# Twenty-seven tiny extra loads in a softmax-attention kernel: fifteen on SyncE near the end, twelve on GpSimd at head 22

## The chip, the cores and the metric

The kernel runs on one core of a Trainium2 chip. The metric is the device time of one launch in microseconds. A profile of a separate execution, taken by the hardware profiler, shows where the time goes; its span is counted from the first to the last instruction.

## What is computed

One decode step of full attention and its gradients, for 32 heads, one query row per head, 8192 keys and values of 128 elements, all in bf16:

```python
def _fwd_reference(q, k, v):
    scale = q.shape[-1] ** -0.5
    scores = jnp.einsum('bhqd,bhkd->bhqk', q, k) * scale
    attn = _softmax(scores, axis=-1)
    return jnp.einsum('bhqk,bhkd->bhqd', attn, v)

def reference(q, k, v, grad_out):
    _out, _vjp = jax.vjp(_fwd_reference, q, k, v)
    return (_out, *_vjp(grad_out))
```

K and V are read once (2 MB a head each) and dK and dV, of the same size, are written once. dV of a head is the outer product of its 8192 probabilities with its row of `grad_out`; dK is that of the 8192 score gradients with its row of `q`. The outputs `out_0` (attention) and `out_1` (dQ) are 8 KB each.

## The kernel before

**Tiles.** A head's K, V, dK or dV is one tile of 128 partitions by 64 rows by 128 elements in bf16: 16 KB a partition, contiguous in memory. There are three buffers for K (`K_BUFS`), two for V (`V_BUFS`), and two each for dK and dV (pool `gen`).

**The loop.** The loop over `h` runs from 0 to 32 and is skewed by one head: in turn `h` the scores, softmax and output of head `h` are computed, and dK and dQ of head `h - 1` are finished. TensorE makes the scores and the contractions, VectorE transposes K blocks in 32x32 squares (`k_blocks`) and makes the outer products (`outer`, a quarter of a tile at a time), ScalarE copies and takes the exponential.

**Order.** From `manual_schedule()` on, every engine's instructions, its queue of transfers too, stand in the order in which the program names them. In a turn, SyncE's queue gets: the load of K of head `h + 2` (L336), the store of dK of head `h - 1` (behind the last quarter, L365), the load of V of head `h + 2` (L390) and the store of dV of head `h` (L391). Head 0 and head 31 store in halves; K of head 0 comes in four pieces. Two transfers are issued by ScalarE: the rows of `q` and `grad_out` at the start (L88, L89). The first load of K, V, K, V (heads 0 and 1, L90 to L93) stands before the hand-made order begins. For the last heads no load is left: V of head 31 is asked for in turn 29. Turn 30 therefore ends with the store of dV of head 30; turn 31 then stores dK of 30, dV of 31 in halves and the attention result (`result`, L395), and turn 32 stores dK of 31 in halves and the dQ result (L397).

**GpSimd** clears some tiles at the start and has nothing to do after that; it issues no transfer.

Lines that matter: L81 loads K, L85 loads V, L266 stores dK and dV, L302 stores a result, L424 is the end of the program.

Of the kernel before, what the change touches and what calls it, by code (L numbers as in the profile page):

```python
# [11 lines left out]
BF16 = mybir.dt.bfloat16  # L12
# [7 lines left out]
K_BUFS = 3  # L20
V_BUFS = 2
QD = 32


@with_exitstack
def kernel(
# [11 lines left out]
    nc = tc.nc  # L38
    P = 128
    _, H, S, D = k.shape  # L40
    assert D == P and S % (P * CH) == 0 and H <= P
    NT = S // P
    NCH = NT // CH
    NQ = P // QD
    assert NCH == 4 and NQ == 4
    W = D // 2
    NB = W // QD
    scale = float(D) ** -0.5
# [8 lines left out]
    single = ctx.enter_context(tc.tile_pool(name="single", bufs=1))  # L57
# [11 lines left out]
    def rows_of(x, h, c, parts):  # L69
        L = NT // parts  # L70
        return x[0, h].rearrange("(p n) d -> p n d", p=P)[:, c * L:(c + 1) * L, :]
# [11 lines left out]
    def load_v(h):  # L83
        Vt[h] = vpool.tile([P, NT, D], BF16, tag="V", name="Vt")
        nc.sync.dma_start(Vt[h][:], rows_of(v, h, 0, 1))  # L85
# [16 lines left out]
    nc.vector.memset(ones_f[:], 1.0)  # L102
    do_win = consts.tile([P, H, 2, QD + 2], BF16)
    nc.gpsimd.memset(do_win[:], 0.0)
    wins = {}
    for which in ("p", "ds"):
        wins[which] = []
        for i in range(2):
            w = consts.tile([P, NG, 2 * QD - 4], BF16, name=f"win_{which}{i}")
            nc.gpsimd.memset(w[:], 0.0)  # L110
            wins[which].append(w)
    q_win = []
    for i in range(2):
        w = consts.tile([P, 2 * NB, P + QD], BF16, name=f"win_q{i}")
        nc.gpsimd.memset(w[:], 0.0)
# [5 lines left out]
    q_blk = consts.tile([P, H, 2 * NB, NQ], BF16)  # L121
    four = consts.tile([H, 2 * NB, NQ, QD], BF16)
    for w in range(NB):
# [33 lines left out]
    def k_blocks(h, u):  # L157


        if u == 0:  # L160
            XK[h] = ktpool.tile([P, CH, NB, NCH, QD], F32, tag="XK", name="XK_sb")
        nc.vector.transpose(XK[h][:, :, :, u, :],  # L162
                            slots(Kt[h], u, NCH).rearrange("p g d -> p (g d)").bitcast(F32).rearrange(
                                "p (g w j) -> p g w j", g=CH, w=NB))

    def q_window(h):
        nc.scalar.copy(q_win[h % 2][:, :, 2 * NCH - 2:2 * NCH - 2 + P].rearrange("p c (a r) -> p c a r", r=QD)[:, :, :, 0],
                       q_blk[:, h])
# [55 lines left out]
    def contract(h, which, first=0, last=NG):  # L224
        X, pool = (Vt[h], psO) if which == "p" else (Kt[h], psQ)
        if h % ST == 0 and first == 0:
            acc[which] = pool.tile([P, 512], F32, tag="acc", name="acc_" + which)
        at = QD - 4 - 4 * (h % ST)
        for g in range(first, last):
            b = g % NQ  # L230
            nc.tensor.matmul(acc[which][b * QD:(b + 1) * QD, :], lhsT=window(h, which)[:, g, at:at + QD],  # L231
                             rhs=X[:, 4 * g:4 * g + 4, :].rearrange("p n d -> p (n d)"),
                             start=(h % ST == 0 and g < NQ), stop=(h % ST == ST - 1 and g >= NG - NQ),
                             skip_group_check=True)
# [33 lines left out]
    def rows_bc(h, bank):  # L268
        nc.tensor.matmul(bank, lhsT=ident[0:H, h:h + 1].to_broadcast([H, P]),
                         rhs=rows[:].rearrange("h a d -> h (a d)"), start=True, stop=True,  # L270
                         skip_group_check=True)
        qd[h] = small.tile([P, 2, D], BF16, tag="qd", name="qd", bufs=3)
        nc.scalar.copy(qd[h][:].rearrange("p a d -> p (a d)"), bank)  # L273

    def pd_sum(h):
        x = st[h]
        nc.tensor.matmul(x["m"][:, 1:2], lhsT=ones_f[:], rhs=x["pd"][:], start=True, stop=True,
                         skip_group_check=True)
# [13 lines left out]
    def dq_of(h, half):  # L292
        contract(h, "ds", half * NG // 2, (half + 1) * NG // 2)

    def result(src, dst):
        half = small.tile([P, H], BF16, tag="half", name="half")
        nc.scalar.copy(half[:], src[:])
        fin_ps = psT.tile([P, 2 * TB, P], BF16, tag="T", name="fin_ps")
        nc.tensor.transpose(fin_ps[0:H, 0, :], half[:], ident[:])
        fin_sb = small.tile([H, D], BF16, tag="fin", name="fin_sb")  # L300
        nc.scalar.copy(fin_sb[:], fin_ps[0:H, 0, :])
        nc.sync.dma_start(dst.rearrange("b h s d -> (b h s) d"), fin_sb[:])  # L302

    for h in range(H + 1):
        p_ = h - 1
        if h < H:
            x = st[h] = {}
            if h == 0:
                q_window(0)
                first = psT.tile([P, 512], F32, tag="T", name="first")  # L310
                rows_bc(0, first[:, 256:512])
            for u in range(NCH - 1):
                k_blocks(h, u)
                k_scores(h, u)
        if h > 0:
            v_back(p_)
            pd_sum(p_)
        if h < H:
            k_blocks(h, NCH - 1)
            k_scores(h, NCH - 1)  # L320
        if h == 0:
            do_columns()
        if h > 0:
            ds_of(p_)
            outer(p_, "dk", 0)
            dq_of(p_, 0)
        if h < H:
            s_back(h)
        if h > 0:
            dq_of(p_, 1)  # L330
            outer(p_, "dk", 1)
            if p_ % ST == ST - 1:
                gather_copy("ds")
                gather(p_, "ds", st[p_]["m"])
        if 0 < h and h + 2 < H:
            load_k(h + 2)  # L336
        if h < H:
            mx = small.tile([P, 1], F32, tag="mx")
            nc.vector.tensor_reduce(mx[:], x["sn"], axis=AX.XY, op=ALU.max)
            top = small.tile([P, 1], F32, tag="top")  # L340
            nc.vector.tensor_scalar_mul(top[:], mx[:], scale)  # L341
            x["m"] = psM.tile([P, 512], F32, tag="m", name="m_ps")
            nc.tensor.transpose(x["m"][:, 128:256], top[:].to_broadcast([P, P]), ident_f[:])  # L343
        if h > 0:
            outer(p_, "dk", 2)
        if h == 0:
            load_k(2)
        if h < H:
            nbias = small.tile([P, 1], F32, tag="nbias")
            nc.vector.tensor_reduce(nbias[:], x["m"][:, 128:256], axis=AX.X, op=ALU.max, negate=True)  # L350
            v_transposes(h, 0)
            v_transposes(h, 1)
            e = x["e"] = small.tile([P, NT], F32, tag="e", name="e")
            rs = small.tile([P, 1], F32, tag="rs")
            nc.scalar.activation(e[:].rearrange("p (u g) -> p u g", u=NCH), x["sn"], ACT.Exp, bias=nbias[:], scale=scale, accum_out=rs[:])  # L355
            nc.tensor.matmul(x["m"][:, 0:1], lhsT=ones_f[:], rhs=rs[:], start=True, stop=True,  # L356
                             skip_group_check=True)
            v_copy(h, 0)
            v_copy(h, 1)
            if h + 1 < H:  # L360
                rows_bc(h + 1, x["m"][:, 256:512])
                q_window(h + 1)
            v_transposes(h, 2)
        if h > 0:
            outer(p_, "dk", 3)  # L365
        if h == H:
            break
        rinv = x["rinv"] = small.tile([P, 1], F32, tag="rinv", name="rinv")
        nc.vector.reciprocal(rinv[:], x["m"][:, 0:1])  # L369
        x["p"] = small.tile([P, NT, R], BF16, tag="prep", name="p_rep")  # L370
        nc.scalar.activation(x["p"][:], e[:].unsqueeze(2).to_broadcast([P, NT, R]), ACT.Copy, scale=rinv[:])  # L371
        nc.scalar.copy(window(h, "p")[:, :, QD - 4:QD], x["p"][:, :, 0].rearrange("p (g j) -> p g j", j=4))  # L372
        x["p_s"] = small.tile([P, NT], F32, tag="p_s", name="p_s")
        nc.vector.tensor_scalar(x["p_s"][:], e[:], rinv[:], scale, op0=ALU.mult, op1=ALU.mult)
        v_copy(h, 2)
        for c in range(3, NX // TB):
            v_transposes(h, c)
            v_copy(h, c)
            if c == 4:
                contract(h, "p")  # L380
        if h % ST == ST - 1:
            gather_copy("p")
        v_scores(h)
        if h % ST == ST - 1:
            gather(h, "p", x["m"])
        outer(h, "dv", 0)
        outer(h, "dv", 1)
        outer(h, "dv", 2)
        if 0 < h and h + 2 < H:
            load_v(h + 2)  # L390
        outer(h, "dv", 3)  # L391
        if h == 0:
            load_v(2)
        if h == H - 1:
            result(o_all, out_0)  # L395

# [32 lines left out]
```

## Time and profile before

| | |
|---|---|
| median of 3 runs | 642.11 us (642.06 to 642.62) |
| the profiled execution | 642.33 us, span 640.5 us |
| bytes moved | 269.01 MB, mean 420 GB/s (134.23 MB read, 134.23 MB written in HBM) |
| busiest engine | VectorE, 546.7 us, 780 instructions |
| K load, 2 MB, issue to landing | 31.6 us median of 31 |
| V load, 2 MB | 29.5 us median of 32 |
| dV store, 2 MB | 34.8 us median of 30 |
| dK store, 2 MB | 32.2 us median of 30 |

How to read it: "busy" of an engine counts its computing instructions only. A transfer is issued by an instruction on a queue (SPq is SyncE's) that takes a fraction of a microsecond; "to landing" is the time from there until all of its data is down and its semaphore is complete. Sixteen DMA engines share the packets of each transfer, and every engine works through its own part of the queue in order. A wait line reads: engine, line that waited, `<-` what it waited for, then microseconds in total, times, and the longest.

### The profile page before, as it was taken

The numbers are of one execution on the slowest core, as the hardware profiler recorded it, in microseconds if no ns is written. First come the engines' busy times: TensorE is split into PE (matmuls) and PEld (weight loads), VectorE is DVE, ScalarE is ACT, GpSimd is POOL, SyncE is SP. The second block draws the span as 40 slices with busy tenths as digits, with TensorE's granted clock in tenths as the row PEclk, the third lists the DMA queues.
The fourth block names the chain that finished last, engine by engine and source line by source line (L and its number), as shares of the span: only waits on it lengthen the run. The fifth ranks groups of instructions, "written<-read, shape, count | busy, mean of one in ns | idle before, by whom it ended". The sixth has DMA issues, their size and how long they took to land.

```text
span 640.5 us, 8426 instructions
## 1 busy us (share of the span) xinstructions
PE 466.5 (73%) x3336; PEld 276.5 (43%) x3336; DVE 546.7 (85%) x780; ACT 205.5 (32%) x507; POOL 7.1 (1%) x13
## 2 busy tenths in 40 slices
PE   3776778778877867887866867767877687676771
PEld 1444444445544533455533444434554344444351
DVE  6799999998999999988889888898888988889871
ACT  1433332234433322334421333313442133322240
POOL 4000000000000000000000000000000000000000
PEclk9979888887787899877899887898787888879875
DMA  8999999999999999999999999999999999999994
GB/s 353 421 415 427 429 431 426 425 433 426 429 431 427 429 431 427 430 429 429 431 427 432 428 425 437 427 424 436 428 425 435 428 426 434 426 430 433 427 405 193
DMA packets 19671, 269.01 MB, mean 420 GB/s; under 512 B 2352, under 2 KB 2352, under 8 KB 2864
## 3 DMA queue, kind: packets, MB, share of 16 engines
q1 hardware_dynamic: 19536, 268.46, 98.6%
q8 instruction: 26, 0.43, 0.3%
q14 instruction: 13, 0.11, 0.0%
q10 hardware_dynamic: 96, 0.02, 0.0%
HBM read 134.23 MB, written 134.23 MB: 419 GB/s over the span
## 4 chain that ended last, share of the span: by engine, by line
DMA 45%; DVE 39%; PE 9%; ACT 4%; issue 1%; DVEq 0%; ACTq 0%
DMA Kt<-in_k_dram 45%; DVE XK_sb L162 15%; DVE G_dv L256 9%; DVE G_dk L256 7%; PE s_ps L177 3%; DVE dpT L214 2%; PE T_ps L197 2%; PE acc_ds L231 2%; ACT XV_sb L188 2%; DVE sT L184 1%; ACT p_rep L371 1%; DVE prod L217 1%; DVE ds L285 1%; ACT qd L273 1%; DVE four L125 1%
## 5 line engine op out<-in xcount | busy, mean ns | idle before, releaser
L197 PE MATMUL T_ps<-ident_f,Vt 128*128 128x128 f32 x1024 | 178.0, 339 | 1.0 <-DMA Vt<-in_v_dram 0.4
L256 DVE TENSOR_TENSOR G_dv<-p_rep,qd 128x2048 bf16<-128x2048 bf16 x128 | 148.2, 1220 | 35.3 <-DMA out_dram<-G_dv 28.1
L177 PE MATMUL s_ps<-XK_sb,win_q 128*128 128x512 bf16 x512 | 135.8, 397 | 50.1 <-DVE XK_sb L162 26.3
L197 PEld LDWEIGHTS T_ps<-ident_f,Vt 128*128 128x128 f32 x1024 | 151.4, 177 | 28.5 <-issue 20.1
L256 DVE TENSOR_TENSOR G_dk<-ds_rep,qd 128x2048 bf16<-128x2048 bf16 x128 | 154.7, 1210 | 1.1
L188 ACT COPY XV_sb<-T_ps 128x512 f32<-128x512 f32 x256 | 138.4, 586 | 53.2 <-PE T_ps L197 52.6
L162 DVE STREAM_TRANSPOSE XK_sb<-Kt 128x1024 f32<-128x1024 f32 x128 | 151.4, 1221 | 3.1 <-DMA Kt<-in_k_dram 2.9
L177 PEld LDWEIGHTS <-win_q 128*128 128x128 bf16 x512 | 52.7, 105 | 123.8 <-issue 83.2
L290 ACT COPY win_ds<-ds 128x64 bf16<-128x64 bf16 x32 | 7.8, 244 | 193.0 <-DVE ds L285 193.0
L355 ACT ACTIVATE e<-sT,nbias 128x64 f32<-128x64 f32 x32 | 13.0, 406 | 138.4 <-DVE nbias L350 138.4
L343 PE MATMUL m_ps<-ident_f,top 128*128 128x128 f32 x32 | 11.0, 342 | 60.3 <-DVE top L341 57.3
L207 PE MATMUL dp_ps<-XV_sb,do_win 128*32 128x512 bf16 x512 | 34.0, 382 | 24.7 <-ACT XV_sb L188 24.7
L231 PE MATMUL acc_p<-Vt,win_p 128*32 128x512 bf16 x512 | 48.3, 516 | 0.5 <-ACT win_p L372 0.5
L343 PEld LDWEIGHTS m_ps<-ident_f,top 128*128 128x128 f32 x32 | 4.5, 139 | 74.4 <-DVE top L341 72.9
L231 PE MATMUL acc_ds<-Kt,win_ds 128*32 128x512 bf16 x512 | 33.5, 382 | 0.9 <-ACT win_ds L290 0.9
L207 PEld LDWEIGHTS <-do_win 128*32 128x32 bf16 x512 | 14.2, 94 | 36.0 <-issue 29.5
L369 DVE RECIPROCAL rinv<-m_ps 128x1 f32<-128x1 f32 x32 | 5.4, 168 | 24.9 <-ACT qd L273 24.9
L184 DVE STREAM_TRANSPOSE sT<-s_ps 128x512 f32<-128x512 f32 x32 | 22.7, 709 | 3.6 <-PE s_ps L177 3.6
L356 PE MATMUL m_ps<-rs,ones_f 128*128 128x1 f32 x64 | 15.4, 310 | 11.5 <-ACT e L355 11.5
L231 PEld LDWEIGHTS <-win_p 128*32 128x32 bf16 x512 | 13.1, 117 | 23.8 <-issue 12.2
L214 DVE STREAM_TRANSPOSE dpT<-dp_ps 128x512 f32<-128x512 f32 x32 | 21.6, 675 | 0.8 <-PE dp_ps L207 0.8
L356 PEld LDWEIGHTS m_ps<-rs,ones_f 128*128 128x128 f32 x64 | 14.0, 272 | 17.8 <-ACT e L355 17.3
(57 smaller groups left out, 203.3 us busy)
## 6 DMA issues: line engine op xcount, KB each, us to landing
Vt<-in_v_dram SPq DMA_DIRECT2D x32, 2048.0 KB, 29.5
Kt<-in_k_dram SPq DMA_DIRECT2D x31, 2048.0 KB, 31.6
out_dram<-G_dv SPq DMA_DIRECT2D x30, 2048.0 KB, 34.8
out_dram<-G_dk SPq DMA_DIRECT2D x30, 2048.0 KB, 32.2
out_dram<-G_dv SPq DMA_DIRECT2D x4, 1024.0 KB, 11.6
out_dram<-G_dk SPq DMA_DIRECT2D x4, 1024.0 KB, 11.7
Kt<-in_k_dram SPq DMA_DIRECT2D x4, 512.0 KB, 5.6
out_dram<-fin_sb SPq DMA_DIRECT2D x2, 8.0 KB, 12.1
```

Source lines behind the costliest of these rows:

```text
L162: nc.vector.transpose(XK[h][:, :, :, u, :], slots(Kt[h], u, NCH).rearrange("p g d -> p (g d)").bitcast(F32).rearrange("p (g w j) -> p g w ...
L177: nc.tensor.matmul(st[h]["s"][:], lhsT=q_win[h % 2][:, c, at:at + P], rhs=cols[:, c // 2, u, c % 2], start=(u == 0 and c == 0), stop=(u == ...
L184: nc.vector.transpose(sT[:].rearrange("p g r -> p (g r)"), x["s"][:])
L188: nc.scalar.copy(XV[h][:, c * TB:(c + 1) * TB, :], st[h].pop(("T", c))[:])
L197: nc.tensor.transpose(T_ps[:, i, :], words[:, m * P:(m + 1) * P], ident_f[:])
L207: nc.tensor.matmul(out[b * QD:(b + 1) * QD, :], lhsT=do_win[:, h, e2, 2 - 2 * z:2 - 2 * z + QD], rhs=cols[:, z, e2, :, b * QD:(b + 1) * QD ...
L214: nc.vector.transpose(x["dpT"][:].rearrange("p m r -> p (m r)"), x["dp"][:])
L231: nc.tensor.matmul(acc[which][b * QD:(b + 1) * QD, :], lhsT=window(h, which)[:, g, at:at + QD], rhs=X[:, 4 * g:4 * g + 4, :].rearrange("p ...
L256: nc.vector.tensor_tensor(slots(G, r, 4).rearrange("p n (a b) -> p n a b", b=R), slots(rep, r, 4).unsqueeze(2).to_broadcast([P, Q, D // R, ...
L343: nc.tensor.transpose(x["m"][:, 128:256], top[:].to_broadcast([P, P]), ident_f[:])
L355: nc.scalar.activation(e[:].rearrange("p (u g) -> p u g", u=NCH), x["sn"], ACT.Exp, bias=nbias[:], scale=scale, accum_out=rs[:])
L356: nc.tensor.matmul(x["m"][:, 0:1], lhsT=ones_f[:], rhs=rs[:], start=True, stop=True, skip_group_check=True)
```

## The change

The kernel gets two helpers and two calls. `marks_sync` makes fifteen loads on SyncE, number `i` over `i` partitions with `i` elements of bf16 (2 to 30 bytes) in each, from the corner of `q`, side by side into columns of one tile of 16 x 120. It is called in turn 30, behind the last quarter of `outer(30, "dv", ...)`. `marks_pool` clears a tile of 128 x 174 on VectorE and makes twelve loads on GpSimd into columns of it, from K of head 0, over 2, 2, 3, 5, 7, 2, 4, 125, 3, 16, 2 and 8 partitions with 9 to 20 elements in each; it is called in turn 22 after dV. Nothing reads either tile. No other line is changed.

```diff
@@ -20,6 +20,7 @@
 QD = 32
+MARKS = (2, 2, 3, 5, 7, 2, 4, 125, 3, 16, 2, 8)
@@ -291,6 +292,20 @@
+    def marks_sync():
+        mark = single.tile([16, 120], BF16, tag="mark_s", name="mark_s")
+        for i in range(1, 16):
+            at = i * (i - 1) // 2
+            nc.sync.dma_start(mark[0:i, at:at + i], q.rearrange("b h s d -> (b h s) d")[0:i, 0:i])
+
+    def marks_pool():
+        mark = single.tile([P, 174], BF16, tag="mark_p", name="mark_p")
+        nc.vector.memset(mark[:], 0.0)
+        words = k[0, 0].rearrange("(p n) d -> p n d", p=P)
+        for i, n in enumerate(MARKS):
+            at = 9 * i + i * (i - 1) // 2
+            nc.gpsimd.dma_start(mark[0:n, at:at + 9 + i], words[0:n, 0, 0:9 + i])
@@ -391,6 +406,10 @@
         outer(h, "dv", 3)
         if h == 0:
             load_v(2)
+        if h == 22:
+            marks_pool()
+        if h == H - 2:
+            marks_sync()
         if h == H - 1:
             result(o_all, out_0)
```

## The prediction, made before the changed kernel ran

> **What bounds the kernel now.** I read the page's table by slices first. It shows transfers busy at nine tenths or more in 38 of the 40 slices, against 85% for the busiest engine, and almost all bytes in SyncE's one queue.
>
> ```profile
> PE 466.5 (73%) x3336; PEld 276.5 (43%) x3336; DVE 546.7 (85%) x780; ACT 205.5 (32%) x507; POOL 7.1 (1%) x13
> ...
> DMA  8999999999999999999999999999999999999994
> ...
> q1 hardware_dynamic: 19536, 268.46, 98.6%
> ```
>
> So the time is the bytes, 268 MB at some 427 GB/s, and a little work on an engine costs nothing while that queue stays filled. Second, SyncE's own instructions in order of time, at the end. Columns: start, duration, line, transfer.
>
> ```profile
> 591.61 0.33 SPq L266 DMA_DIRECT2D out_dram<-G_dk  x1
> 599.24 0.33 SPq L266 DMA_DIRECT2D out_dram<-G_dv  x1
> 611.45 0.33 SPq L266 DMA_DIRECT2D out_dram<-G_dk  x1
> 616.84 2.60 SPq L266 DMA_DIRECT2D out_dram<-G_dv  x2
> 621.87 0.34 SPq L302 DMA_DIRECT2D out_dram<-fin_sb  x1
> 625.21 2.60 SPq L266 DMA_DIRECT2D out_dram<-G_dk  x2
> 627.90 0.40 SPq L302 DMA_DIRECT2D out_dram<-fin_sb  x1
> ```
>
> The row at 599.24 is dV of head 30; the new SyncE loads stand between it and dK of head 30 at 611.45. Third, the view of transfers, asked for the one microsecond in which that dV was issued, and the stretches of the tail (length, busy time of each engine, clock, DMA share, GB/s).
>
> ```profile
> out_dram<-G_dv SPq DMA_DIRECT2D x1, 2048.0 KB, 25.3
> ```
>
> ```profile
> 620.00:625.00 5.00, 2.89 (x30) 1.94 (x29) 3.75 (x8) 1.47 (x5) 0.00 (x0) 0.91 0.84 353
> 625.00:630.00 5.00, 1.69 (x8) 1.40 (x8) 2.45 (x3) 0.64 (x3) 0.00 (x0) 0.50 0.94 394
> 630.00:635.00 5.00, 0.00 (x0) 0.00 (x0) 0.00 (x0) 0.00 (x0) 0.00 (x0) 0.50 0.44 180
> 635.00:640.50 5.50, 0.00 (x0) 0.00 (x0) 0.00 (x0) 0.00 (x0) 0.00 (x0) 0.50 0.04 18
> ```
>
> That dV lands at 599.24 + 25.3 = 624.5. The last result is issued at 627.90 and, by the 11.6 of its line's fastest landing, is down at 639.5. From 630 on, fewer and fewer of the 16 DMA engines work: the end is set by the slowest of them, which empties a backlog. After 624.5 it has dK of 30, dV of 31, dK of 31 (2 MB each) and 8 KB to write, which takes it 15.0 us, near three times the 4.9 of 2 MB at 427 GB/s. Fourth, SyncE's waits in the first 7 us, and the instructions of the store line.
>
> ```profile
> 0.74 1.80 SPq L81 DMA_DIRECT2D Kt<-in_k_dram  x4
> ...
> 4.08 0.45 SPq L85 DMA_DIRECT2D Vt<-in_v_dram  x1
> 5.08 0.33 SPq L81 DMA_DIRECT2D Kt<-in_k_dram  x1
> ```
>
> ```profile
> SPq L81 <- DMA Kt<-in_k_dram: 0.5, 1, 0.5
> SPq L266 <- DMA rows<-in_grad_out_dram: 0.4, 1, 0.4
> ```
>
> ```profile
> L266 SPq EVENT_SEMAPHORE  x68: 17/17/17, 5.9 to 625.6; - x68
> ```
>
> This is the view that decides the forecast. The load at 5.08 is K of head 2: the third of three K buffers, so no data holds it, and yet it waited 0.5 us for a K transfer. It is the tenth transfer of the two hardware queues; the second is the first piece of K of head 0. The next wait is that of the first dV store, the eleventh, for the load of grad_out, about the third. Neither touches the other's data. And all 68 stores have a wait instruction ahead of them beside the wait of the store itself, which is for VectorE. I read this as a rotation of eight completion semaphores over the transfers of SyncE and ScalarE: each issue waits until the transfer eight places earlier has landed. In the steady part it costs nothing: 4 transfers in 19.8 us a head and 30 to 35 us to landing are six to seven in flight.
>
> **The change, part by part.** Nothing is removed or moved. (1) Fifteen SyncE loads, s1 to s15, behind the dV at 599.24. By the rotation s1 to s3 wait for transfers already down. s4 waits for dK of 28 (issued 571.82, 32.6 to landing: 604.4), s5 for V of 31 (578.10 + 31.2 = 609.3), s6 for dV of 29 (579.42 + 34.9 = 614.3), s7 for dK of 29 (591.61 + 27.8 = 619.4), s8 for dV of 30: 624.5. s9 to s15 wait for s1 to s7, which are in the queue behind that same dV and need no longer. dK of 30 stands behind all of them and waits for s8 itself. So it goes out not at 611.45 but after 624.5, when the queue is empty.
>
> The price of the hole: an issue costs 0.45 (the four of K of head 0, 1.80 in all); s8 to s15 are 8 x 0.45 = 3.6, so dK of 30 is issued at 624.5 + 3.6 = 628.1. s8 itself lands before that: the 8 KB load of q on an idle queue took 3.2, giving 627.7. From the first issue at 0.74 to the first packet (slice 36 of 40 when the first 2 us are asked for) is 1.0. Before, the slowest engine went on without a break: its last packet of dV of 30 ended some 0.65 before its landing (packets of the last result stop at about 638.85 and it lands at 639.5). So the hole runs from 623.9 to 629.1, 5.2 us. Behind it come the same 15.0 us; by 629 dV and dK of 31 are long computed or nearly so (both gradients' buffers are released by stores issued before the loads), so SyncE issues the rest without a pause.
> Bounds: issue at the 0.33 of the bare instruction makes the landing of s8 decide, 627.7 instead of 628.1, -0.4, and another -0.5 if these few bytes land faster than 8 KB; issue at the 0.8 of V of head 0 (2.58 to 3.42) makes 8 x 0.84 = 6.7, +3.1. I take 0.45: same queue, nothing waiting.
>
> (2) Twelve GpSimd loads at head 22, 179 rows in all. No GpSimd transfer is in the trace, so it is bounded: GpSimd has 7.1 us of work, over by 8 us, and nobody reads the tile, so its waits hold up nobody. What counts is the time of the slowest DMA engine, which has no slack to the end. From below 0: most engines are through by 632 and have over 7 us to spare. From above: the small result of 621.87 + 12.7 lands 0.2 after the half store ahead of it (619.11 + 15.3 = 634.4), 12 x 0.2 = 2.4. I take 0.3, nearer the 96 packets of ScalarE's two small loads, which show as 0.0% of the span. (3) The memset of 128x174 on VectorE: at most the 0.3 of the 128x256 copy of ds; hidden by the gap of 1 to 2 us that VectorE has in every head. (4) At the end SyncE must also see GpSimd's eight or so counts; its end waits at L424 are 28 ns each in the median: 0 to 0.3, I take 0.2.
>
> Sum: 5.2 + 0.3 + 0.2 = 5.7. The profiled execution took 642.33 (span 640.5, 1.8 around it), 0.2 over the median of 642.11: 642.33 + 5.7 = 648.0.
>
> A rule against it: the Trainium skill, "DMA: Bandwidth & Descriptors", section "Issuing engines are not separate DMA queues", says that issue time on a sequencer is usually small beside the transfer; by that the fifteen cost 15 x 0.45 = 6.8 us inside a gap of 11.9 and the sum would be 642.8. The row of K of head 2 is of another kind, a wait and not an issue, and I go by it. The same page, section on why a DMA increments its semaphore by 16, asks for one semaphore per transfer in flight, since two in flight on one cannot be told apart; that would be the reason of such a wait.
>
> **The rivals.** A, not slower: the two waits at the start are something else, and the loads fit between 599.57 and 611.45, where 15 x 0.45 = 6.8 of 11.9 us are used. Then only (2) to (4) are left: 642.33 + 0.3 (0 to 0.8) = 642.6. It decides if dK of 30 is still issued near 611.5. For it: in the whole steady part no wait of SyncE for a transfer is listed. Against it: the 68 extra wait instructions.
> B: GpSimd's loads draw on the same eight semaphores. Then SyncE runs dry at head 22 as well, and a second hole of about 5.2 gives 648.0 + 5.2 = 653.2. For it: ScalarE's two loads share the rotation. Against it: GpSimd's queue does not occur in the trace, so nothing shows sharing.
> C: the tiny loads go one at a time, each waiting for the one before in the same tile. s8 to s15 then need 8 x 3.2 = 25.6 instead of 3.6: 648.0 + 22 = 670. Against it: the four pieces of K of head 0 go into one tile 0.45 apart.
>
> **How the numbers follow.** The main case 80%, A 12%, B 5%, C 3%. Main range: 648.0 - 0.9 - 0.5 = 646.6 to 648.0 + 3.1 + 2.2 = 653.3, which takes in B. Below I leave 1.1 for a hole that faster engines shorten. 645.5 to 653.5 leaves out A, C and a little of the main case. 0.2% is 1.3 us, about what a measurement here can tell from no change. Slower: main, B and C, 88%. Same: A but for 1%. Faster: 1%.
>
> **What would show it.** Step by step: a wait of SyncE for the landing of dV of 30 or of a tiny load in the tail; the eighth tiny load at about 624.5; dK of 30 at 627 to 629; a slice of the tail with the DMA share near zero; an unchanged steady part up to 599 (within 1 us, else the GpSimd part is mis-sized). I am wrong if dK of 30 leaves near 611.5, if SyncE pauses at head 22, or if the tiny loads are spaced by their landings.

## The result, and the profile after

The changed kernel takes 647.11 us (median of 3, 647.09 to 647.25) against 642.11 before: 1.0076 times, 95% interval 1.0053 to 1.0099. Its profiled execution took 647.25 with a span of 645.5, so 4.9 more than the one before. In the page's table by slices, the two rows on transfers, and the list of queues:

```profile
DMA  8999999999999999999999999999999999999928
GB/s 348 421 429 427 426 431 424 431 421 433 428 429 428 427 431 427 431 428 429 427 434 425 434 425 432 428 430 423 432 427 428 430 430 426 432 426 433 423 115 358
...
q1 hardware_dynamic: 19776, 268.46, 97.8%
...
q0 software_dynamic: 384, 0.01, 0.0%
```

The steady part is as before. New is one slice near the end, the 39th, with 115 GB/s, and a last slice that is busy where it used to trail off. GpSimd's loads are a queue of their own (q0) and take 0.0% of the span.

SyncE's instructions in order of time (start, duration, line, transfer, count):

```profile
599.32 0.33 SPq L267 DMA_DIRECT2D out_dram<-G_dv  x1
...
604.50 0.25 SPq L300 DMA_DIRECT2D mark_s<-in_q_dram  x1
609.38 0.26 SPq L300 DMA_DIRECT2D mark_s<-in_q_dram  x1
614.44 0.27 SPq L300 DMA_DIRECT2D mark_s<-in_q_dram  x1
619.59 0.27 SPq L300 DMA_DIRECT2D mark_s<-in_q_dram  x1
624.61 2.97 SPq L300 DMA_DIRECT2D mark_s<-in_q_dram  x8
627.67 0.37 SPq L267 DMA_DIRECT2D out_dram<-G_dk  x1
628.14 1.33 SPq L267 DMA_DIRECT2D out_dram<-G_dv  x2
```

Its waits in the tail (line, what it waited for, us in total, times, longest):

```profile
SPq L300 <- DMA out_dram<-G_dv: 9.5, 2, 4.8
...
SPq L300 <- DMA out_dram<-G_dk: 8.7, 2, 4.9
...
SPq L300 <- DMA Vt<-in_v_dram: 4.6, 1, 4.6
```

Five tiny loads of `q` (s4 to s8) wait for stores of dK and dV and a load of V, none of which they touch. dK of head 30 leaves at 627.67 where it left at 611.45.

The trace settles what they wait on: its record of every issuing instruction names the semaphore that the transfer completes on. SyncE's and ScalarE's transfers take the numbers 100, 102 to 107 and 109 in turn, eight in all, before and after the change. dV of head 30, s8 and dK of head 30 have the same one, 104, eight places apart, and s8's own instruction waits on 104. The twelve GpSimd loads use eight others, 111 to 118.

The stretches of the tail (length, busy time by engine, clock, DMA share, GB/s), and transfers from 624 to 629 in 40 slices (each 0.125 us):

```profile
620.00:624.00 4.00, 2.40 (x19) 0.80 (x19) 3.33 (x8) 1.08 (x3) 0.00 (x0) 0.62 0.06 25
624.00:629.00 5.00, 2.16 (x9) 1.88 (x9) 2.08 (x2) 0.64 (x3) 0.00 (x0) 0.50 0.14 53
629.00:634.00 5.00, 0.00 (x0) 0.00 (x0) 0.00 (x0) 0.00 (x0) 0.00 (x0) 0.50 1.00 419
634.00:639.00 5.00, 0.00 (x0) 0.00 (x0) 0.00 (x0) 0.00 (x0) 0.00 (x0) 0.50 1.02 421
```

```profile
DMA  0000000000000000000000000000000000009900
```

From 620 to 624 one engine in sixteen (share 0.06) still writes dV of head 30; the others have run out, since dK of 30 is not there. Then nothing until slice 37, some 0.9 after dK of 30 is issued. After that all sixteen write side by side, at 419 to 421 GB/s. By the trace's packet records the 16 KB packets end at 624.1 and begin again at 628.5: a hole of 4.45 us on the engine that sets the end.

### The profile page after: what moved, and what is told of

Read it like the earlier page. It is cut to its first block, busy times and chain, and to the rows that moved or that the text cites. A ratio compares the mean times of both kernels' runs of the same rounds, so it can differ in the third digit from the quotient of the medians.

```text
span 645.5 us, 8458 instructions
## 1 busy us (share of the span) xinstructions
PE 471.4 (73%) x3336; PEld 274.9 (43%) x3336; DVE 545.2 (84%) x781; ACT 204.7 (32%) x507; POOL 13.7 (2%) x25
## 4 chain that ended last, share of the span: by engine, by line
DMA 49%; DVE 29%; PE 14%; ACT 3%; issue 1%; DVEq 0%; ACTq 0%
DMA Kt<-in_k_dram 49%; DVE XK_sb L163 11%; PE s_ps L178 7%; DVE G_dv L257 6%; DVE G_dk L257 6%; PE T_ps L198 2%; PE acc_ds L232 2%; DVE dpT L215 1%; ACT XV_sb L189 1%; DVE sT L185 1%; ACT p_rep L386 1%; PE m_ps L371 1%; PE acc_p L232 1%; PE m_ps L246 1%; DVE ds L286 1%
## 5 line engine op out<-in xcount | busy, mean ns | idle before, releaser
L178 PE MATMUL s_ps<-XK_sb,win_q 128*128 128x512 bf16 x512 | 145.6, 424 | 42.3 <-DVE XK_sb L163 24.4
L198 PE MATMUL T_ps<-ident_f,Vt 128*128 128x128 f32 x1024 | 173.7, 333 | 1.5 <-DMA Vt<-in_v_dram 1.0
L198 PEld LDWEIGHTS T_ps<-ident_f,Vt 128*128 128x128 f32 x1024 | 147.7, 173 | 28.3 <-issue 19.8
L178 PEld LDWEIGHTS <-win_q 128*128 128x128 bf16 x512 | 54.6, 110 | 121.1 <-issue 85.4
```

The costliest lines, as they stand in the source:

```text
L178: nc.tensor.matmul(st[h]["s"][:], lhsT=q_win[h % 2][:, c, at:at + P], rhs=cols[:, c // 2, u, c % 2], start=(u == 0 and c == 0), stop=(u == ...
L198: nc.tensor.transpose(T_ps[:, i, :], words[:, m * P:(m + 1) * P], ident_f[:])
```

## The experiments

My theory: SyncE's and ScalarE's transfers share eight completion semaphores in rotation; an issue waits until the transfer eight places earlier has landed; fifteen tiny loads behind one large store therefore make SyncE wait until that store has landed, and the queue runs dry for the issues that are still left. Rivals are named with each run. Ratios are to the kernel before on the same chip (medians of before 642.39 to 642.65); other edits are relative to the changed kernel. Runs without the GpSimd loads leave out only loads that nobody reads.

**Each half alone.**

```diff
-        if h == 22:
-            marks_pool()
```

> The fifteen SyncE loads alone, no GpSimd loads. Theory 1 (eight completion semaphores in rotation, so the queue runs dry at dV of head 30): nearly the whole cost stays, 642.1 + 4.4 to 4.8 = 646.5 to 646.9, dK of head 30 issued within 0.2 us of 627.6, the 16 KB packets pausing for 4.4 to 4.5 us. Rival (the GpSimd loads at head 22 made the slow DMA engine late): 642.3 to 643.5.

646.90, 1.0068 (1.0053 to 1.0083). The 16 KB packets pause for 4.47, and SyncE's two lines are as in the changed kernel (dK of head 30 is 0.23 ahead of the expected 627.6; dV of head 30, at 599.06, is 0.26 ahead of the changed kernel's):

```profile
599.44 27.83 SPq L300 DMA_DIRECT2D mark_s<-in_q_dram  x15
627.37 0.37 SPq L267 DMA_DIRECT2D out_dram<-G_dk  x1
```

```diff
-        if h == H - 2:
-            marks_sync()
```

> The twelve GpSimd loads alone. Theory 1: 642.1 + 0.2 to 0.4 (some 0.1 in the queue, 0.26 in the end waits) = 642.3 to 642.5. Rival (GpSimd loads draw on the same semaphores, or slow the DMA engines): 644 or more.

642.91, 1.0006 (0.9996 to 1.0015). The SyncE loads are the cost; the GpSimd loads are at most some 1 us, and no effect is clear. The median lies above the expected 642.5, but so does that of before on this chip, 642.65.

**How many loads.** Six, seven and thirty in place of fifteen, without the GpSimd loads.

```diff
-        for i in range(1, 16):
+        for i in range(1, 7):
```

> Six SyncE loads (i = 1 to 6) in place of fifteen, no GpSimd loads. Theory 1: dK of head 30 is then eight places behind dK of head 29, goes out at that landing, near 619.5, while the slowest DMA engine still has dV of 30 to write; no hole: 642.0 to 642.4. Rival (a price per load, 4.7 us for fifteen): 642.1 + 1.9 = 644.0.

642.39, 0.9999 (0.9989 to 1.0009). The 16 KB packets don't pause.

```diff
-        for i in range(1, 16):
+        for i in range(1, 8):
```

> Seven SyncE loads (i = 1 to 7), no GpSimd loads. Theory 1: dK of head 30 is eight places behind dV of head 30 itself and goes out at that landing, near 624.6; first packet 0.9 later, against a last packet of dV at 624.1: a hole of 1.4, 643.3 to 643.7. Rival (a price per load): 642.1 + 2.2 = 644.3, and no step of over 1 us between six and seven loads.

644.28, 1.0027 (1.0018 to 1.0037): 1.6 us by medians, 1.7 by the ratio, where the theory had 1.2 to 1.6 and a pause of 1.4 (measured 1.44). The median is 0.58 above the theory's range, and 0.54 of that is this chip's baseline, 642.65 instead of 642.1. By its time alone this run doesn't fell the rival, whose 644.3 it meets; the step from six to seven does. SyncE's instructions with six loads, then with seven:

```profile
599.35 14.96 SPq L300 DMA_DIRECT2D mark_s<-in_q_dram  x6
619.24 0.37 SPq L267 DMA_DIRECT2D out_dram<-G_dk  x1
```

```profile
599.98 20.11 SPq L300 DMA_DIRECT2D mark_s<-in_q_dram  x7
624.89 0.38 SPq L267 DMA_DIRECT2D out_dram<-G_dk  x1
```

One load more moves dK of head 30 from the landing of one large store (dK of 29) to that of the next (dV of 30), over 5 us on. By the semaphores on record, it shares that of dK of 29 (103) with six loads and that of dV of 30 (104) with seven. With six, SyncE waits too, but the slowest DMA engine still has dV of 30 to write, and nothing is lost. A price per load can't make such a step, and the step stands where a rotation of eight puts it. (With six loads the 1.9 us of that rival lie outside the interval.)

Thirty, the fifteen more in the same tile, which is widened to 270 columns:

```diff
+        for i in range(15):
+            nc.sync.dma_start(mark[0:15, 120 + 10 * i:130 + 10 * i], q.rearrange("b h s d -> (b h s) d")[0:15, 0:10])
```

> The fifteen SyncE loads and fifteen more of 15 rows behind them, no GpSimd loads. Theory 1 with the hole made of the issues that still stand behind dV's landing: 15 more issues at the 0.48 us from the last 15-row load to dK of 30 in the changed kernel make 7.2 us more: dK of 30 issued near 634.8, time 646.9 + 7.2 = 654.1 (653 to 655). Rival (the hole is one round of draining and refilling, whatever stands behind the eighth load): 646.5 to 647.5.

653.64, 1.0170 (1.0155 to 1.0185).

```profile
627.73 6.63 SPq L302 DMA_DIRECT2D mark_s<-in_q_dram  x15
634.46 0.37 SPq L267 DMA_DIRECT2D out_dram<-G_dk  x1
```

The fifteen more take 6.73 us of SyncE, 0.45 each, and the time is 6.7 above that with fifteen. Past the step, the hole is made of issue time, one for one. In the tail the pause of the 16 KB packets is the cost: none, 1.44, 4.47 and 11.14 with six, seven, fifteen and thirty loads, against none, 1.6, 4.2 and 11.1 by medians.

**Another queue.** The fifteen loads from GpSimd and from ScalarE, at the same place in the program.

```diff
-            nc.sync.dma_start(mark[0:i, at:at + i], q.rearrange("b h s d -> (b h s) d")[0:i, 0:i])
+            nc.gpsimd.dma_start(mark[0:i, at:at + i], q.rearrange("b h s d -> (b h s) d")[0:i, 0:i])
```

> The same fifteen loads at the same place, issued by GpSimd in place of SyncE; no loads at head 22. Theory 1 with separate semaphores for GpSimd: SyncE's order is that of before, dK of 30 at 611.5, 642.3 to 642.9. Rival (the fifteen transfers themselves, their bytes and completions in the DMA engines, make the hole): 645 or more.

642.76, 1.0001 (0.9991 to 1.0011). But this didn't test what it was meant to: GpSimd has no other work and these loads wait for no data, so they ran between 7.9 and 20.4 us, not in the tail. Hence the same with something to hold them:

```diff
+        nc.vector.memset(mark[:], 0.0)
         for i in range(1, 16):
```

> The fifteen loads from GpSimd, held back to turn 30 by a memset of their tile on VectorE in that turn (in the run from GpSimd before this one nothing held them, and they ran in the first 20 us). Theory 1: they run near 599, SyncE issues dK of head 30 near 611.5 as before, 642.3 to 643.2. Rival (the transfers themselves, issued in the tail, make the hole): 645 or more.

642.77, 1.0006 (0.9996 to 1.0015). GpSimd's first eight loads and its ninth, and SyncE's dK of head 30:

```profile
599.41 4.22 POOL L301 DMA_DIRECT2D mark_s<-in_q_dram  x8 [591.44 <-DVE mark_s L298]
605.58 0.52 POOL L301 DMA_DIRECT2D mark_s<-in_q_dram  x1 [1.95 <-DMA mark_s<-in_q_dram]
```

```profile
611.47 0.33 SPq L267 DMA_DIRECT2D out_dram<-G_dk  x1
```

The same transfers, issued in the tail too (599.4 to 612.8), and SyncE's order is that of before. So it is not the transfers, and GpSimd's completions are not in SyncE's rotation. They have one of their own, semaphores 111 to 118 on record, and the ninth load, which has the first one's semaphore, waits for a landing; that holds up nobody.

```diff
-            nc.sync.dma_start(mark[0:i, at:at + i], q.rearrange("b h s d -> (b h s) d")[0:i, 0:i])
+            nc.scalar.dma_start(mark[0:i, at:at + i], q.rearrange("b h s d -> (b h s) d")[0:i, 0:i])
```

> The same fifteen loads issued by ScalarE in place of SyncE; no loads at head 22. Theory 1 with the rotation common to SyncE and ScalarE: ScalarE itself is held until dV of 30 has landed, near 627.6, and the 22 us of work that stood between its copy of win_ds (605.3) and the last dK store (627.5) begin only then: 652 to 656. Rival (each queue has a rotation of its own): 642.1 to 643.5.

647.92, 1.0080 (1.0061 to 1.0099): slower, so the rotation is common to both queues, but the 652 to 656 were wrong. SyncE's waits, and its instructions:

```profile
SPq L267 <- DMA mark_s<-in_q_dram: 30.1, 1, 30.1
...
SPq L86 <- DMA mark_s<-in_q_dram: 6.5, 1, 6.5
```

```profile
567.05 0.34 SPq L82 DMA_DIRECT2D Kt<-in_k_dram  x1
597.57 0.33 SPq L267 DMA_DIRECT2D out_dram<-G_dk  x1
604.50 0.34 SPq L86 DMA_DIRECT2D Vt<-in_v_dram  x1
```

A SyncE store of dK waits 30.1 us for a load on ScalarE's queue that it shares nothing with but the rotation. I had expected ScalarE to be held behind dV of 30. It was the other way round. The places in the rotation stand in the program (each instruction has its semaphore); by the semaphores on record ten of the tiny loads got theirs ahead of dK of head 28, which has the third one's (102), and SyncE stood until ScalarE came to them, from 595.5 on.

**Another place.** The fifteen behind dV of head 22, in the middle:

```diff
-        if h == H - 2:
+        if h == 22:
             marks_sync()
```

> The fifteen SyncE loads behind dV of head 22 in place of head 30; no GpSimd loads. Theory 1: the queue runs dry there as well, near 475, and what the bound resource lost does not come back: 642.1 + 4.4 to 5.5 = 646.5 to 647.6, with one pause of the 16 KB packets of 4 to 5 us in the middle. Rival (the hole costs only in the tail, where no loads are left; in the middle the work behind it makes up for it): 642.1 to 643.5.

649.39, 1.0104 (1.0089 to 1.0120): the hole costs there too (the rival falls), 6.85 by medians, 2.6 more than in the tail (2.3 by the ratios). The 16 KB packets pause for 4.8, within the 4 to 5 expected, so some 2.0 of the cost lies behind the pause. In this run the first large transfer behind it is a load of K. My first explanation was the restart on a load; moving the call behind the load of K of head 25 puts a store there:

```diff
+        if h == 23:
+            marks_sync()
         if h < H:
             mx = small.tile([P, 1], F32, tag="mx")
```

> The fifteen SyncE loads in turn 23 behind the load of K of head 25, so that the first large transfer behind them is the store of dK of head 22, where the run at head 22 had the load of K of head 25. Theory 1a (the excess over the tail's hole there, 6.85 against 4.4, is the restart on a load, whose first packets come late, and the compute that waits for that K): 642.5 + 4.4 to 5.2 = 646.9 to 647.7. Rival 1b (a hole in the middle costs more than one in the tail whatever stands behind it): 649 or more.

649.30, 1.0105 (1.0090 to 1.0120), with a pause of 4.7: that explanation falls. The stretches behind its pause, and three of the same ones in the kernel before:

```profile
484.00:488.00 4.00, 2.80 (x25) 1.02 (x23) 2.10 (x7) 0.24 (x1) 0.00 (x0) 1.00 1.05 422
488.00:490.00 2.00, 0.00 (x0) 0.00 (x0) 0.00 (x0) 0.00 (x0) 0.00 (x0) 1.00 0.97 270
490.00:492.00 2.00, 0.00 (x0) 0.00 (x0) 1.07 (x1) 0.00 (x0) 0.00 (x0) 0.61 0.95 401
492.00:494.00 2.00, 0.00 (x0) 0.00 (x0) 2.00 (x4) 0.00 (x0) 0.00 (x0) 0.50 1.08 352
494.00:496.00 2.00, 0.48 (x1) 0.18 (x1) 1.97 (x5) 0.39 (x2) 0.00 (x0) 0.50 0.94 262
```

```profile
488.00:490.00 2.00, 0.18 (x1) 0.13 (x1) 1.97 (x5) 0.00 (x0) 0.00 (x0) 1.00 0.96 410
...
492.00:494.00 2.00, 2.00 (x11) 1.76 (x11) 0.65 (x3) 1.78 (x6) 0.00 (x0) 0.50 1.13 483
494.00:496.00 2.00, 2.00 (x24) 1.19 (x24) 0.41 (x1) 1.67 (x4) 0.00 (x0) 0.91 0.97 401
```

The DMA engines are busy throughout (the last column but one) and yet move 262 to 352 GB/s in three of the stretches, against 401 to 483 before: about 2 us worth of bytes. I took the slow stretches for the first packets of the next two loads, which all sixteen engines reach together behind a hole. In step they are: the sixteen counts on the semaphore of the first load behind this hole (V, issued at 483.82) land from 496.08 to 496.80, where those of a load in the steady part before (K, issued at 487.67) land from 510.70 to 520.16.

But the place doesn't fit. A 2 MB transfer is 128 packets of 16 KB, which take 0.61 us each in the steady part. Taken from the hole on in lots of sixteen, in order of time, the slow ones here are the last two lots of the store of dK (0.83 and 1.23 us a packet in the mean) and the last four of the load of V (0.70, 0.88, 1.27, 0.76); the first lots of that load take 0.61 to 0.65. In the run at head 22 they are the first two and the last two lots of the first load (1.41 and 0.73, 0.87 and 0.96), and the next load, two transfers later, has none. In the tail of the changed kernel, with stores alone, no lot of dK of head 30 takes more than 0.64. What slows them stays open.

The last run asks whether the loss is the same behind a short hole, with seven loads at head 22:

```diff
-        for i in range(1, 16):
+        for i in range(1, 8):
```

> Seven SyncE loads behind dV of head 22 in place of fifteen; no GpSimd loads. In the tail seven cost 1.7 and fifteen 4.4; in the middle fifteen cost 6.85, 2.0 more than their hole of 4.9. Theory (behind any hole the 16 DMA engines start in step, and the next two loads from HBM then begin slowly; the excess doesn't grow with the hole): hole 1.4 to 1.7 and the same 2.0 on top, 642.5 + 3.4 to 3.7 = 645.9 to 646.2. Rival (the excess is in proportion to the hole, 6.85 / 4.4): 642.5 + 2.6 = 645.1 or less.

645.52, 1.0056 (1.0043 to 1.0070), so 3.1 by medians and 3.6 by the ratio, with a pause of 1.5 in the packets. By the ratio this is the theory's 3.4 to 3.7 and the proportional 2.6 is just outside the interval; by the median it is below the range I gave. The packets speak for an excess that doesn't grow with the hole: the eight lots of the first load take 1.5 us more than at 0.61 each behind this pause and 1.6 behind the one of 4.8. The theory's cause, engines in step at the beginnings of two loads, isn't shown: here too the slow lots are the first two and the last few of one load.

**Spread out.** One of the fifteen behind the dV store of each turn from 16 to 30 (the helper makes load number `h - 15` alone):

```diff
-        if h == H - 2:
-            marks_sync()
+        if 16 <= h < H - 1:
+            marks_sync(h)
```

> The same fifteen SyncE loads, one behind the dV store of each turn from 16 to 30; no GpSimd loads. Theory 1: five transfers a turn then share the eight semaphores, so SyncE waits for landings in the steady part, but a backlog of about 6 large transfers stays in the queue and it never runs dry: 642.1 to 642.9, no pause of the 16 KB packets. Rival (each wait for a landing costs by itself, or each tiny load does): 643.5 or more.

642.53, 0.9999 (0.9990 to 1.0009). SyncE's waits in the whole run, largest for a landing first, and the transfers from 430 to 600:

```profile
SPq L301 <- DMA out_dram<-G_dk: 59.7, 13, 4.8
SPq L267 <- DMA out_dram<-G_dv: 58.5, 13, 4.7
SPq L82 <- DMA Vt<-in_v_dram: 54.9, 12, 4.6
```

```profile
DMA  9999999999999999999999999999999999999999
```

Over 170 us of waits for landings in these three lines alone, no pause of the 16 KB packets, and nothing lost that could be measured. In these runs a wait of SyncE costs only when the queue behind it empties.

## Why the prediction was right

It gave 648.0, with 645.5 to 653.5, and slower at 88%. Measured: 647.11.

- **The wait, and which transfer ends it.** s4 to s8 were expected at 604.4, 609.3, 614.3, 619.4 and 624.5 and left at 604.50, 609.38, 614.44, 619.59 and 624.61. The 0.5 us wait of one load at the start of the trace carried the forecast. Six against seven loads and the semaphores on record show the eight.
- **The hole**, 5.2 predicted, 4.45 measured: the largest error. The issue was set at 0.45, from loads over 128 partitions; s8 to s15 and the way to dK of 30 took 3.06, 0.38 each, since an issue of few rows is shorter (0.25 for 4 rows, 0.38 for 15). That is 0.5 of the 0.75. The first packet came 0.9 after the issue rather than 1.0, and the last packet of dV of 30 ended at 624.1 rather than 623.9, 0.5 before its landing rather than 0.65. The landing of s8, set at 3.2 after its issue, took 1.27 (its last count is at 625.88) and never decided.
- **The rest behind it**, 15.0 predicted: 15.2 from the first packet of dK of 30 to the last packet. Sixteen engines side by side (419 to 421 GB/s) write each at about the pace that the slowest had alone (25 GB/s).
- **GpSimd's loads**, 0.3: alone they are 1.0006, and the interval holds 1, so no run shows this term. dV of 30 left 0.1 later than before, which is less than executions differ by (599.06 with the SyncE loads alone). At the end SyncE has 11 wait instructions where it had 7, and from the trace's last landing to the end of the span it is 1.26 against 1.06: 0.2, as predicted (1.20 with the GpSimd loads alone, 1.00 with the SyncE loads alone).
- Sum of what the two profiled executions show: 4.45 + 0.2 + 0.1 + 0.2 = 4.95, against 4.9 between them and 5.0 by medians. All four terms come from the same two traces, so that they add up proves nothing further.
- **The rivals.** A (the loads fit in a gap) falls with dK of 30 at 627.67; its 642.6 was also 0.2 short of its own terms (2) to (4), 0.3 and 0.2. With it falls the sum drawn from the Trainium skill's remark that issue time is usually small beside the transfer ("DMA: Bandwidth & Descriptors", "Issuing engines are not separate DMA queues"): the issues are short, 0.25 to 0.38 each, and six loads cost nothing (0.9999), but for fifteen that sum leaves out the wait. B (GpSimd in the same rotation) falls with the held GpSimd loads. C (one at a time) falls with the 0.31 to 0.41 from one to the next of s8 to s15.

One thing the prediction had too simply: it priced the hole as if its place made no difference. In the tail that is so, with only stores left. In the middle the same fifteen cost 6.85.

## What to carry to other kernels

In a kernel bound by transfers, count what is in flight against the semaphores that completions rotate through, here eight for SyncE and ScalarE together. Here a burst of seven or more small transfers between two large stores held the second until the first had landed, however few bytes they were, and emptied the queue. Spreading such loads over the loop, or issuing them from GpSimd, cost nothing that could be measured here. A wait at the issuing queue is not itself a loss; look for a stretch in which the DMA share falls towards zero.

## What the runs showed that I had not expected

- The DMA engines can be busy and slow: behind a hole in the middle, 262 GB/s at a DMA share of 0.94. Why is open.
- An empty queue, once refilled with stores, is at full rate at once (419 GB/s from 629 on).
- Transfers of two queues can wait for each other through the rotation alone, for 30.1 us with ScalarE's loads, and in an order that is not that of the program's lines.
- GpSimd's twelve loads, of 3.9 KB at most, took 5.9 to 10.1 us from issue to landing beside the busy SyncE queue, without slowing it by anything that could be measured.
